# Two batches' loads cut into half-runs, and three loads issued later on GpSimd, in a cosine-weighted attention with adapter mixture

## The chip, the cores and the metric

The kernel runs on one core of one Trainium2 chip. The metric is the device time of one execution in microseconds (us); lower is better. Three runs of the kernel before gave 114.01, 114.30 and 114.53 us, so its median is 114.30 us.

## What is computed

Queries, keys and values have shape 8 x 8 x 576 x 64 (batch, heads, tokens, head size), in float32. Each batch goes through linear attention with cosine weights, and the 4608 tokens that come out, each of 512 numbers, go through a layer that picks the best two of eight small adapters:

```python
cos_w, sin_w = cos(pi/2 * pos / 576), sin(pi/2 * pos / 576)
phi(x) = concat([relu(x) * cos_w, relu(x) * sin_w])
kv  = einsum('bhsf,bhsd->bhfd', phi(k), v)      # 128 x 64 per head
z   = sum(phi(k), over s)
x   = (phi(q) @ kv) / (phi(q) @ z + 1e-6)       # tokens x 512
w   = softmax of the two largest of x @ w_gate  # 8 experts
out = x + sum over the two experts of w * (x @ A[e] @ B[e])
```

## The kernel before

**Batches and steps.** A batch's attention needs the whole of its keys and values first: `kv` sums over all its tokens. Only then can its queries be used. The kernel holds one batch as tiles of 128 partitions by 4 head pairs by 9 times 64 numbers: `rows` gives partition r of an even or odd head the nine tokens 9r to 9r+8, which lie next to each other in memory. So one load of k, q or v is 128 x 4 = 512 runs of 2304 bytes (576 float32 numbers), written as 1152 bytes of bfloat16. The nine tokens of a run are the "s values" 0 to 8 of the code.

The output is made in 36 tiles of 128 tokens. One loop, `for n in range(NT - 1)`, has a step for each tile; every engine runs its part of the step in the order in which the code writes it (the schedule is manual). Two batches share nine tiles. In step n VectorE (DVE) normalises tile n, TensorE (PE) transposes the queries of tile n+1, ScalarE (ACT) evacuates them, and the adapter stages of earlier tiles are mixed in.

**Keys.** Before PE can use the keys of a batch, each s value is turned into two scaled copies (`kp`, by cosine and sine). For batches 2 to 7 this is shared: DVE takes relu of the first part in place (`relu_k`, L165), GpSimd (POOL) then scales these s values two instructions each (L156, a "row" of GpSimd), DVE and ACT scale the rest from the raw keys (L153, L151). `pool_at`, `relu_at`, `dve_at` and `act_at` say in which step: batch 2 in step 5 with five s values on GpSimd, batch 3 in step 8 with seven, batch 4 in step 12 with eight, batch 5 in step 17 with eight, batches 6 and 7 in steps 20 and 23 with nine. In steps 5 and 8 DVE scales s value 7 first, by two L153 instructions, and then takes the two relus. PE uses the `kp` tiles in `kv` (L180), for batch 3 in the order 7, 0 | 1, 2, 3 | 4, 8, 6, 5 over steps 10, 11 and 12.

**Loads.** All loads but the first (batch 0's keys, on SyncE's queue) are issued by GpSimd, since they convert float32 to bfloat16. They use one DMA queue and land in the order of issue. In the built program the DMA starts of GpSimd take eight semaphores in turn, and each start waits until the eighth start before it has landed; GpSimd's later work stands behind such a wait. The order before is: v0, q0, k1, v1, q1, k2, three transfers of weights (A, w_gate and B, `load_weights`), v2, q2, k3, v3, k4, q3, v4, all written ahead of the loop; then behind each row of GpSimd the loads k(b+3), q(b+2), v(b+3). Here "k3" is batch 3's keys. The third and fourth batch of the change are batches 2 and 3 by this count.

**Stores.** SyncE waits for the last keys' load (`first_loads`, L570), stores the tiles held until then, and stores the others as they are made.

Of the kernel before, what the change touches and what calls it, by code (L numbers as in the profile page):

```python
# [19 lines left out]
def kernel(ctx, tc, q, k, v, w_gate, A, Bw, out):  # L20
# [27 lines left out]
    def rows(dram, b):  # L48
        return dram[b].rearrange("(g two) (r s) d -> (two r) g (s d)", two=2, s=NS)
# [9 lines left out]
    v_b += v_b[:3]  # L59

    def load(eng, t, dram, b):
        eng.dma_start(out=t, in_=rows(dram, b))  # L62

    def load_k(b, eng=None):
        load(eng or nc.gpsimd, k_b[b].rearrange("p g s d -> p g (s d)"), k, b)

    def load_q(b):
        load(nc.gpsimd, q_b[b].rearrange("p g s d -> p g (s d)"), q, b)

    def load_v(b):  # L70
        load(nc.gpsimd, v_b[b][:, 0:VN].rearrange("p (g x) -> p g x", g=G), v, b)
# [36 lines left out]
    def make_diag(s):  # L108
        for i, tab in enumerate((cos_tab, sin_tab)):
            nc.vector.tensor_scalar(out=diag[:, s, i], in0=ident, scalar1=tab[:, s:s + 1],  # L110
                                    scalar2=None, op0=ALU.mult)
# [6 lines left out]
    def load_weights():  # L118
        nc.gpsimd.dma_start(out=AW[:, 0:E].rearrange("p e c r -> p e (c r)"),
                            in_=A.rearrange("e (p c) r -> p e (c r)", c=DCH))  # L120
        nc.gpsimd.dma_start(out=AW[:, E, :, 0:E],
                            in_=w_gate.rearrange("(p c) e -> p c e", c=DCH))
        nc.gpsimd.dma_start(out=Ball, in_=Bw.rearrange("e r d -> (e r) d"))
# [35 lines left out]
    def scale_k(b, s, eng=("pool", "pool")):  # L159
        for i, e in enumerate(eng):  # L160
            scale_k1(b, s, i, e)
# [13 lines left out]
    def kv(b, s):  # L175
        first, last = kv_n[b] == 0, kv_n[b] == NS - 1
        kv_n[b] += 1
        for g in range(G):
            for par, pr in enumerate((lo, hi)):
                nc.tensor.matmul(out=kvz[par][:, g], lhsT=kp_t[b][pr, s, g],  # L180
                                 rhs=v_rhs(b, g, s, pr),
                                 start=(first and g == 0), stop=(last and g == G - 1))

    def kv_out(b):
        kv_t[b] = t = p_kv.tile([128, 2, G, W], BF16, name="kvsb")
        for par in range(2):
            src = kvz[par].rearrange("p g u d -> p g (u d)")[:, :, 0:W]
            nc.scalar.copy(t[:, par], src)
# [29 lines left out]
    def evac_q(n, gp, eng="act"):  # L218

        t = p_qpt.tile([128, 4, 128], BF16, name="qpT")  # L220
        src, qpT_t[n, gp] = qpT_t[n, gp], t
        if mixed(n):
            src = src.rearrange("p j h r -> p h j r")
            t = t.rearrange("p h (j r) -> p h j r", j=2)
        else:
            src = src.rearrange("p j h r -> p h r j")
            t = t.rearrange("p h (r j) -> p h r j", j=2)
        if eng == "act":
            nc.scalar.activation(t, src, AF.Relu)  # L229
        else:  # L230
            nc.vector.tensor_scalar(out=t, in0=src, scalar1=0.0, scalar2=None, op0=ALU.max)  # L231

    def move_q(n):
        transp_q(n)
        evac_q(n, 0)
        evac_q(n, 1)
# [148 lines left out]
    def delta(n, own=True):  # L385
        delta_x(n, own)
        delta_z(n)

    def delta_add(n, own=True):

        if own:
            dx = cd[dx_n[0] % 2]
            dx_n[0] += 1
        else:
            dx = qd.tile([128, DM], FP32, name="dx", tag="qd")
        g = group_of[n]
        nc.tensor.matmul(out=dx, lhsT=zgT_t[g][:, n - groups[g][0], :], rhs=Ball,
                         start=True, stop=True)
        osb_t[n] = dx
        evac_o(n)  # L400
        t = osb_t[n]
        nc.gpsimd.tensor_tensor(out=t, in0=t, in1=xt_t.pop(n), op=ALU.add)  # L402
# [77 lines left out]
    with tc.manual_schedule():  # L480
        for s in range(6):
            make_diag(s)
        wu = qd.tile([128, DM], FP32, name="wu", tag="qd")
        for i in range(24):
            nc.tensor.matmul(out=wu, lhsT=ones, rhs=wide, start=True, stop=True)  # L485
        for s in range(NS):
            scale_k(0, s, ("act" if s < 7 else "dve", "dve"))
            kv(0, s)
        nc.scalar.activation(warm, halfpi, AF.Sigmoid)
        for s in range(6, NS):  # L490
            make_diag(s)
        load_k(1)
        load_v(1)
        load_q(1)
        load_k(2)
        load_weights()
        load_v(2)
        load_q(2)
        load_k(3)
        load_v(3)  # L500
        load_k(4)
        load_q(3)
        load_v(4)
        kv_out(0)
        transp_q(0)
        evac_q(0, 0, "dve")
        evac_q(0, 1)
        numden(0)

        g10, g11, g12 = range(len(groups) - 3, len(groups))  # L510
        todo, held = [], []
        first_loads = persist.tile([1, 8], BF16, name="first_loads")

        def emit(d, own=True, eng="act", add=False):
            if add:
                delta_add(d, own)
            else:
                delta(d, own)
                evac_o(d, eng)
            if held is None:  # L520
                store(d)
            else:
                held.append(d)

        for n in range(NT - 1):
            if n > 0:
                g = move_at.get(n - 1, (None,))[0]
                evac_x(n - 1, g)
                if g is not None:
                    todo += groups[g]  # L530
            normalise(n)
            if n != 3:
                move_q(n + 1)
            for b, s in kv_at.get(n, ()):
                kv(b, s)
                if kv_n[b] == NS:
                    kv_out(b)
            for t in early_at.get(n, ()):
                logits(t)
            if n == 3:  # L540
                move_q(n + 1)
            for g in gate_a_at.get(n, ()):
                gate_a(g)
            for g in gate_b_at.get(n, ()):
                gate_b(g)
            now = todo[:2 if len(todo) > 3 and n not in kv_at else 1]
            del todo[:len(now)]
            for d in now:
                emit(d, n not in kv_at, add=n > 27)
            for g in gate_a_at.get(n, ()):  # L550
                gate_sig(g)
            transp_x(n)
            for g in move_at.get(n, ()):
                transp_z(g)
            for b, s, i in dve_at.get(n, ()):
                scale_k1(b, s, i, "dve")
            for b, s0, s1 in relu_at.get(n, ()):
                relu_k(b, s0, s1)
            for b, s in pool_at.get(n, ()):
                scale_k(b, s)  # L560
                if (b, s) == pool_at[n][-1]:
                    if b + 3 < B:
                        load_k(b + 3)
                    if b + 2 < B:
                        load_q(b + 2)
                    if b + 3 < B:
                        load_v(b + 3)
                    if b + 3 == B - 1:

                        nc.sync.dma_start(out=first_loads, in_=k_b[B - 1][0:1, 0, 0, 0:8])  # L570
                        for d in held:
                            store(d)
                        held = None
            for t in late_at.get(n, ()):
                logits(t)
            numden(n + 1)
            for b, s, i in act_at.get(n, ()):
                scale_k1(b, s, i, "act")


        evac_x(NT - 2)
        normalise(NT - 1)
        transp_z(g10)
        logits(NT - 2)
        evac_z(g10, [("act", 0, 3)])
        todo += groups[g10]
        for d in todo[:-3]:
            emit(d)
        transp_x(NT - 1)
        gate_a(g11)  # L590
        emit(todo[-3])
        gate_sig(g11)
        evac_x(NT - 1)
        logits(NT - 1)
        gate_b(g11)
        emit(todo[-2])
        gate_a(g12)
        transp_z(g11)
        evac_z(g11, [("act", 0, 2)])
        gate_sig(g12)  # L600
        emit(todo[-1])
        gate_b(g12)
        emit(NT - 3)
        transp_z(g12)
        evac_z(g12, [("dve", 0, 1)])
        emit(NT - 2)
        emit(NT - 1, eng="dve")
# [28 lines left out]
```

## Time and profile before

| | before |
|---|---|
| median of three runs | 114.30 us (114.01 to 114.53) |
| the profiled execution, its own time | 114.54 us |
| its span, first to last instruction | 112.8 us |
| granted TensorE clock | 0.996 |
| PE busy | 96.1 us (85%) |
| DVE busy | 83.7 us (74%) |
| ACT busy | 78.2 us (69%) |
| POOL busy | 72.3 us (64%) |
| GpSimd's DMA queue | 13856 packets, 13.84 MB |
| SyncE's DMA queue | 5792 packets, 10.62 MB |

Busy times leave out waiting and the issuing of DMAs where the profile gives that to a queue; GpSimd's own DMA starts (about 0.75 us each) are counted as busy. A busy PE is not PE at its peak. Times in the views count from the first instruction; 1.7 us of the execution lie outside the span.

### The profile page before, as it was taken

How to read it: one execution, taken by the hardware profiler on the slowest of the kernel's cores; microseconds unless marked ns; L12 is line 12 of the kernel's file. 1: busy time of each engine (PE TensorE's matmuls, PEld its weight loads, DVE VectorE, ACT ScalarE, POOL GpSimd, SP SyncE). 2: the span in 40 equal slices, each digit the busy share in tenths (PEclk: the TensorE clock that was granted, in tenths of full speed). 3: DMA queues.
4: the chain of work that ended last, by engine and by line, in shares of the span. 5: the costliest groups of instructions: out<-in, count | busy, mean ns of one | idle time of the engine just before them, and what ended most of it. 6: DMA issues, size and time to landing. Idle time of an engine off the chain costs nothing.

```text
span 112.8 us, 4956 instructions
## 1 busy us (share of the span) xinstructions
PE 96.1 (85%) x2050; PEld 74.1 (66%) x2068; DVE 83.7 (74%) x296; ACT 78.2 (69%) x169; POOL 72.3 (64%) x134
## 2 busy tenths in 40 slices
PE   2999676978899899999999999998998997978710
PEld 1347465867796788868788888785786886754200
DVE  5598489459969677695987998999949589786620
ACT  5087579755986595797876978856777777895720
POOL 5992223228995996299939999989980445774000
PEclk9999999999999999999999999999999999999998
DMA  2999999999999999999999999999999424526892
GB/s 41 385 206 208 213 202 210 210 180 208 208 208 209 207 209 209 209 206 213 204 207 208 208 209 208 242 348 383 381 324 366 142 100 97 185 101 226 285 340 82
DMA packets 19670, 24.77 MB, mean 220 GB/s; under 512 B 2624, under 2 KB 14528, under 8 KB 19648
## 3 DMA queue, kind: packets, MB, share of 16 engines
q0 software_dynamic: 13856, 13.84, 73.8%
q1 hardware_dynamic: 5792, 10.62, 26.9%
q8 instruction: 16, 0.26, 0.9%
q14 instruction: 6, 0.05, 0.1%
HBM read 28.85 MB, written 9.44 MB: 340 GB/s over the span
## 4 chain that ended last, share of the span: by engine, by line
PE 40%; DMA 28%; DVE 15%; issue 4%; POOL 4%; ACT 4%; POOLq 0%; DVEq 0%; ACTq 0%
DMA k<-in_k_dram 14%; DMA v<-in_v_dram 12%; PE cd L180 9%; PE za L311 7%; PE qd L213 6%; PE xz L285 5%; PE nd L257 4%; DVE xt L277 4%; PE dx L377 3%; DVE k L165 3%; DVE xT L291 2%; DVE zg L346 2%; ACT osb L408 2%; PE qd L201 2%; DMA out_dram<-osb 2%
## 5 line engine op out<-in xcount | busy, mean ns | idle before, releaser
L229 ACT ACTIVATE qpT<-qd 128x512 bf16<-128x512 f32 x71 | 38.6, 595 | 15.0 <-PE qd L213 10.9
L156 POOL TENSOR_SCALAR kp<-k,cos_tab 128x256 bf16<-128x256 bf16 x46 | 22.6, 490 | 7.1 <-DVE k L165 6.5
L277 DVE TENSOR_TENSOR xt<-nd,rden 128x512 bf16<-128x512 f32 x36 | 24.9, 691 | 1.3
L291 DVE COPY xT<-xz 128x512 bf16<-128x512 bf16 (+1 forms) x36 | 17.1, 476 | 9.9 <-PE xz L359 6.4
L156 POOL TENSOR_SCALAR kp<-k,sin_tab 128x256 bf16<-128x256 bf16 x46 | 21.9, 476 | 0.0
L180 PE MATMUL cd<-v,kp 64*128 64x128 bf16 x576 | 20.3, 217 | 0.9 <-DVE kp L153 0.9
L285 PEld LDWEIGHTS <-xt 128*128 128x128 bf16 x144 | 10.8, 115 | 12.1 <-DVE xt L277 7.9
L285 PE MATMUL xz<-ident,xt 128*128 128x128 bf16 x144 | 14.4, 222 | 5.0 <-DVE xt L277 4.3
L180 PEld LDWEIGHTS <-kp 64*128 64x128 bf16 x576 | 16.3, 94 | 3.1 <-issue 0.9
L257 PE MATMUL nd<-kvsb,qpT 128*128 128x65 bf16 (+1 forms) x320 | 16.7, 195 | 1.1 <-DVE qpT L231 0.5
L213 PE MATMUL qd<-diag,q 128*64 128x128 bf16 x432 | 17.3, 222 | 0.3 <-DMA q<-in_q_dram 0.3
L402 POOL TENSOR_TENSOR osb<-osb,xt 128x512 f32<-128x512 f32 x8 | 9.2, 1160 | 9.6 <-ACT osb L408 8.0
L408 ACT COPY osb<-dx 128x512 f32<-128x512 f32 x19 | 11.2, 588 | 5.9 <-remote 2.1
L213 PEld LDWEIGHTS <-q 128*64 128x64 bf16 x432 | 13.1, 109 | 1.8 <-DMA q<-in_q_dram 0.5
L257 PEld LDWEIGHTS <-qpT 128*128 128x128 bf16 (+1 forms) x320 | 12.7, 100 | 1.9 <-ACT qpT L229 0.7
L311 PE MATMUL za<-AW,xT 128*128 128x144 bf16 x140 | 12.4, 227 | 0.7 <-DVE zg L346 0.5
L311 PEld LDWEIGHTS <-xT 128*128 128x128 bf16 x144 | 9.0, 98 | 3.2 <-DVE xT L291 1.0
L408 ACT COPY osb<-cd 128x512 f32<-128x512 f32 x16 | 9.1, 597 | 1.3 <-PE cd L382 1.3
L62 POOL DMA_DIRECT2D v<-in_v_dram x8 | 6.2, 778 | 5.2 <-DMA q<-in_q_dram 4.4
L485 PE MATMUL wu<-wide,ones 128*128 128x512 bf16 x24 | 7.3, 477 | 2.0 <-DVE AW L115 2.0
L62 POOL DMA_DIRECT2D q<-in_q_dram x8 | 6.1, 763 | 3.6 <-DMA k<-in_k_dram 3.6
L62 POOL DMA_DIRECT2D k<-in_k_dram x7 | 5.4, 771 | 3.9 <-DMA k<-in_k_dram 2.2
(75 smaller groups left out, 133.8 us busy)
## 6 DMA issues: line engine op xcount, KB each, us to landing
out_dram<-osb SPq DMA_DIRECT2D x32, 256.0 KB, 3.9
v<-in_v_dram POOLq DMA_DIRECT2D x8, 576.0 KB, 16.5
q<-in_q_dram POOLq DMA_DIRECT2D x8, 576.0 KB, 15.6
k<-in_k_dram POOLq DMA_DIRECT2D x7, 576.0 KB, 15.5
k0f<-in_k_dram SPq DMA_DIRECT2D x1, 1152.0 KB, 5.4
out_dram<-osb SPq DMA_DIRECT2D x8, 128.0 KB, 2.4
AW<-in_moe_A_dram POOLq DMA_DIRECT2D x1, 128.0 KB, 18.2
Ball<-in_moe_B_dram POOLq DMA_DIRECT2D x1, 128.0 KB, 16.7
```

The source lines that it names most:

```text
L62: eng.dma_start(out=t, in_=rows(dram, b))
L156: nc.gpsimd.tensor_scalar(out=dst, in0=src, scalar1=tab, scalar2=1.0, op0=ALU.mult, op1=ALU.mult)
L180: nc.tensor.matmul(out=kvz[par][:, g], lhsT=kp_t[b][pr, s, g], rhs=v_rhs(b, g, s, pr), start=(first and g == 0), stop=(last and g == G - 1))
L213: nc.tensor.matmul(out=t[cols, j, 2 * gi:2 * gi + 2, :], lhsT=q_b[b][:, 2 * gp + gi, s, :], rhs=diag[:, s, i], start=(j == 0 and gi == 0), ...
L229: nc.scalar.activation(t, src, AF.Relu)
L257: nc.tensor.matmul(out=nd[pr, gg, j * W:(j + 1) * W], lhsT=qpT[:, j, pr], rhs=kv_t[b][:, h % 2, h // 2, :], start=(eps_dve(n) and j == 0), ...
L277: nc.vector.tensor_tensor(out=x, in0=nd[:, :, :, 0:D], in1=rden.rearrange("p (g j) -> p g j", g=2).to_broadcast([128, 2, 4, D]), op=ALU.mult)
L285: nc.tensor.transpose(out=xz[:, c * 128:(c + 1) * 128], in_=x[:, c], identity=ident)
L291: nc.vector.tensor_copy(t[:, 0:c], xz[:, 0:c * 128].rearrange("p (c s) -> p c s", c=c))
L311: nc.tensor.matmul(out=za_t[g][:, i, :], lhsT=xT[:, c, :], rhs=AW[:, :, c, :], start=(c == 0 and i == 0), stop=(c == DCH - 1), skip_group_ ...
L402: nc.gpsimd.tensor_tensor(out=t, in0=t, in1=xt_t.pop(n), op=ALU.add)
L408: nc.scalar.copy(t, src)
```

## The change

A load of batch 2 or 3 becomes two transfers. Each takes one half of every run: 512 pieces of 1152 bytes read and 576 written, first the numbers 0 to 287 of all runs (s values 0 to 3 and half of 4), then the others. This touches k2, v2, q2, k3, v3 and q3. The loads k4, q3 and v4 are taken from the list ahead of the loop and put behind GpSimd's row of batch 2, in step 5, ahead of the loads k5, q4 and v5 that stood there already.

GpSimd's order in the changed program: v0, q0, k1, v1, q1, k2 (two), A, w_gate, B, v2 (two), q2 (two), k3 (two), v3 (two); row of batch 2; k4, q3 (two), v4, k5, q4, v5; row of batch 3; the rest as before. The waits on the eighth start before stay and count the halves singly. DVE, ACT and PE keep their instructions and their order; what needs s values of one half only waits for that half.

```diff
     def load(eng, t, dram, b):
-        eng.dma_start(out=t, in_=rows(dram, b))
+        x = rows(dram, b)
+        if b in (2, 3):
+
+            t = t.rearrange("p g (h x) -> p h g x", h=2)
+            x = x.rearrange("p g (h x) -> p h g x", h=2)
+            for h in range(2):
+                eng.dma_start(out=t[:, h], in_=x[:, h])
+        else:
+            eng.dma_start(out=t, in_=x)
...
         load_q(2)
         load_k(3)
         load_v(3)
-        load_k(4)
-        load_q(3)
-        load_v(4)
         kv_out(0)
...
             for b, s in pool_at.get(n, ()):
                 scale_k(b, s)
                 if (b, s) == pool_at[n][-1]:
+                    if b == 2:
+                        load_k(4)
+                        load_q(3)
+                        load_v(4)
                     if b + 3 < B:
                         load_k(b + 3)
```

## The prediction

> **What bounds the kernel now.** I read the page first (engines, DMA, chain), then the chain of waits in order of time, then the stretches, then the timelines around the change. From the page:
>
> ```profile
> DMA  2999999999999999999999999999999424526892
> GB/s 41 385 206 208 213 202 210 210 180 208 208 208 209 207 209 209 209 206 213 204 207 208 208 209 208 242 348 383 381 324 366 142 100 97 185 101 226 285 340 82
> DMA packets 19670, 24.77 MB, mean 220 GB/s; under 512 B 2624, under 2 KB 14528, under 8 KB 19648
> ```
>
> Each figure stands for 2.82 us. From about 5.6 us to 70 us the DMA engines never pause, at a level 208 GB/s; one slice is at 180. A load of 576 KB (589,824 bytes) thus passes every 2.84 us, and each lands that much behind the one before it. The chain, in order of time, shows when this queue sets the pace:
>
> ```profile
> 4.62 13.85 DMA v<-in_v_dram
> 18.76 15.64 DMA k<-in_k_dram
> 34.42 0.48 DVE kp L153 x2
> 34.90 0.60 DVE k L165 x2
> 35.51 0.53 DVE xT L291
> ```
>
> The chain lies on loads until 34.40 us, when k3 lands and DVE, which scales k3's s value 7 first in step 8, can go on. What the wait itself is worth is in the waits of 26 to 36 us:
>
> ```profile
> DVE kp L153 <- DMA k<-in_k_dram: 0.2, 1, 0.2
> POOL kp L156 <- DVE k L165: 1.7, 2, 1.2
> ```
>
> DVE stood idle for only 0.2 us there. An earlier k3 brings 0.2 us at most, a later k3 costs all its delay. Behind that point the stretches say that nothing takes up such a delay:
>
> ```profile
> 20.00:22.50 2.50, 2.37 (x69) 1.99 (x65) 1.30 (x4) 1.84 (x6) 0.74 (x1) 1.00 1.22 213
> 22.50:25.40 2.90, 2.06 (x55) 1.73 (x57) 1.64 (x5) 1.71 (x4) 0.82 (x2) 1.00 1.78 180
> 25.40:30.00 4.60, 3.67 (x88) 3.15 (x82) 4.26 (x19) 3.17 (x8) 4.15 (x9) 1.00 1.21 207
> 40.00:50.00 10.00, 9.83 (x207) 7.78 (x209) 7.60 (x28) 7.61 (x18) 6.85 (x13) 1.00 1.21 208
> 60.00:70.00 10.00, 9.80 (x211) 8.10 (x212) 8.97 (x33) 7.68 (x18) 9.96 (x22) 1.00 1.21 207
> ```
>
> Columns: length; busy us of PE, weight loads, DVE, ACT, POOL; clock; DMA share; GB/s. From 40 us PE is busy 9.8 of every 10 us, in a fixed order, so what PE starts later ends later.
>
> **The half-runs on the DMA queue.** The bytes stay; k2, v2, q2, k3 ahead of k3's landing, and v3 and q3 behind it, take 512 more packets each, 32 on each of 16 engines. No packet of 576 bytes is in the trace. The nearest rows are the small ones of the weights:
>
> ```profile
> AW<-in_moe_A_dram POOLq DMA_DIRECT2D x1, 128.0 KB, 18.2
> AW<-in_moe_w_gate_dram POOLq DMA_DIRECT2D x1, 8.0 KB, 17.5
> ```
>
> A comes in runs of 64 numbers (128 bytes written), so 1024 packets; w_gate in runs of 8 (16 bytes), so 512. Both pass in the stretch 22.5 to 25.4, which moved 2.9 x 180 = 522 KB; at 208 GB/s that takes 2.51 us, so 0.39 us went to 1536 small packets, 96 on each engine: 4.1 ns for each. 32 of them make 0.13 us for a split load. Had the weights' 139 KB (0.67 us at 208 GB/s) cost nothing, it would be (0.39 + 0.67) / 96 = 11 ns, or 0.36 us. Zero is the other end: the same bytes at the same rate. I take 0.2 us, nearer to 0.13 since the small packets' bytes must have cost something. Four splits put k3's second half at 34.40 + 0.8 = 35.2 us; the ends are 34.4 and 35.8. s value 7 lies in the second half, so the early first half of k3 serves nobody: DVE waits in order for 7 before its relus. q2's and v2's first halves do land earlier, but the rows between 26 and 36 us hold no wait for q or v, so that gains nothing.
>
> The Trainium skill has a rule that speaks against the halves ("DMA: Bandwidth & Descriptors", How a descriptor splits into AXI transactions): a piece that does not begin on a 256-byte boundary pays for the bytes below its start. By that page's counting a run of 2304 bytes is 72 beats and its halves 36 and 40, an estimate of 4/72 of 2.84 us or 0.16 us more per split load, beside any cost per packet; four of them would put the sum 0.6 us higher. No run here shows it, since no row of this trace has such a start.
>
> **The three loads moved, and GpSimd's time.** GpSimd's timeline before:
>
> ```profile
> 24.53 0.74 POOL L62 DMA_DIRECT2D k<-in_k_dram  x1 [2.19 <-DMA k<-in_k_dram]
> 25.32 0.74 POOL L62 DMA_DIRECT2D q<-in_q_dram  x1
> 26.06 0.75 POOL L62 DMA_DIRECT2D v<-in_v_dram  x1
> 27.25 0.48 POOL L156 TENSOR_SCALAR kp<-k,cos_tab 128x256 bf16<-128x256 bf16 x1 [0.45 <-DVE k L165]
> 31.36 0.47 POOL L156 TENSOR_SCALAR kp<-k,sin_tab 128x256 bf16<-128x256 bf16 x1
> 33.30 0.76 POOL L62 DMA_DIRECT2D v<-in_v_dram  x1
> 35.28 0.58 POOL L156 TENSOR_SCALAR kp<-k,cos_tab 128x256 bf16<-128x256 bf16 x1 [1.21 <-DVE k L165]
> 41.30 0.48 POOL L156 TENSOR_SCALAR kp<-k,sin_tab 128x256 bf16<-128x256 bf16 x1
> 47.15 0.64 POOL L156 TENSOR_SCALAR kp<-k,cos_tab 128x256 bf16<-128x256 bf16 x1 [3.15 <-DVE k L165]
> ```
>
> Before, row 2 (from 27.25 us) stands behind 16 DMA starts; k4, the 14th, had to wait until the sixth, k2, landed. After, it stands behind 18: three go, five halves come. So the move does not free GpSimd. k3's first half is now the 15th start and waits for the seventh, k2's second half: 24.53 + 0.2 = 24.7 us; three more starts of 0.75 us (the last waits for B, which lands just before v2 begins, three loads ahead of k3: 34.40 - 3 x 2.84 = 25.9, plus 0.2 for k2, no hindrance) end at 27.7. Row 2 starts at 27.75 instead of 27.25 and ends at 32.3. Then come seven starts instead of three: k4 32.3, q3 33.05 and 33.8, v4 34.55, k5 35.3, q4 36.05, and v5, which waits for the eighth before it, v3's first half: 35.2 + 1.5 = 36.7, so it ends at 37.6. Row 3 starts at 37.7 instead of 35.28, 2.4 us late.
>
> Who waits for that? The DMA queue does not run dry: at 32.3 us, with k4's start, it still has k3 and v3 before it, to about 38. Row 4 waited 3.15 us for DVE before: row 3 now ends at 44.2, and its three loads at 46.5, still ahead of 47.15. PE is next, with batch 3's products:
>
> ```profile
> 33.10 1.29 PE L180 MATMUL cd<-v,kp 64*128 64x128 bf16 x40
> 39.32 0.62 PE L180 MATMUL cd<-v,kp 64*128 64x128 bf16 x16
> 41.69 0.84 PE L180 MATMUL cd<-v,kp 64*128 64x128 bf16 x24
> 44.59 1.07 PE L180 MATMUL cd<-v,kp 64*128 64x128 bf16 x32
> ```
>
> An s value is two instructions of 0.46 us on GpSimd and eight matmuls on PE. Batch 3: s value 0 is ready at 37.7 + 1.0 = 38.7, wanted behind 7 at 39.6; 3 at 41.4, wanted at 42.2; 6 at 44.2, wanted behind 4 and 8 at 45.1. Batch 2: 4 at 32.3, wanted behind 3 at 33.4. All hold by 0.8 us or more, and PE will itself be later. So the late rows cost nothing, while that cover of about 0.8 us lasts.
>
> **DVE beside GpSimd's DMA starts.** DVE's short instructions on bfloat16 in SBUF slow down while GpSimd works:
>
> ```profile
> 26.16 0.28 DVE L153 TENSOR_SCALAR kp<-k,cos_tab 128x256 bf16<-128x256 bf16 x1
> 26.35 0.51 DVE L153 TENSOR_SCALAR kp<-k,sin_tab 128x256 bf16<-128x256 bf16 x1
> 34.62 0.28 DVE L153 TENSOR_SCALAR kp<-k,sin_tab 128x256 bf16<-128x256 bf16 x1
> 34.82 0.69 DVE L165 TENSOR_SCALAR k<-k 128x768 bf16<-128x768 bf16 x2
> 65.87 1.30 DVE L165 TENSOR_SCALAR k<-k 128x768 bf16<-128x768 bf16 x2
> 73.57 2.36 DVE L165 TENSOR_SCALAR k<-k 128x768 bf16<-128x768 bf16 x2
> ```
>
> One instruction of two took 0.51 instead of 0.28 us beside v4's start at 26.06; in step 8 (34.42 on) GpSimd was idle, v5's start having ended at 34.06, and nothing was slowed. After, step 8's four instructions, from 35.2 on, run beside the starts of k5 and q4. Two starts at 0.23 us each are 0.46; none is the lower end; 1.30 against 0.69, the pair that met a start and a row, gives 0.6 as the upper. I take 0.3, on the path, right behind k3's wait. Step 5's four meet one start more than before (0.2), but that is ahead of k3's wait and hidden in it. The 2.36 us at 73.57 lie beside row 6 on GpSimd. That row follows row 5 without a gap (POOL busy 9.96 of 10 us from 60 on), and row 5 waits for DVE's own relu of step 17; both shift together, so I leave it.
>
> **The sum.** 0.8 (0 to 1.4) and 0.3 (0 to 0.6): +1.1 us, ends 0 and 2.0. On the profiled execution, 114.54 us (112.8 span and 1.7 around it), that is 115.6; on the median of the runs, 114.3, which lies 0.24 lower, it is 115.4. The queue ends 1.2 us later, six splits at 0.2, and the held stores with it; SyncE stored earlier tiles then, and PE's order does not wait for them.
>
> **Rivals.** *No change.* Half packets cost only their bytes, and DVE slips between the starts: 114.3 us. For it: the queue moves 213 and 207 GB/s around small packets. Against: the 180 slice. 114.1 to 114.8.
>
> *Faster.* k2's and k3's halves and a later k4 would have to free something on the path. The wait for k3 gives back 0.2 us and step 5's slowed instructions 0.2 more, if k3 came 0.4 us earlier: 113.9. It decides if half packets flow faster than whole ones; no row says so. A larger gain needs the 2.36 us at 73.57 to fall to about 1.0, if row 6 ended 1.4 us sooner against DVE: 113.0.
>
> *GpSimd's rows bind.* If GpSimd's starts take longer or its waits stack up, so that row 3 starts over 0.8 us behind my 37.7 with PE on its old times, PE waits for `kp` in steps 10 to 12. A row that starts two more us late gives about 1.2 us on top: 116.6. For it: the eight in flight are now halves. Against: every wait above ends before GpSimd gets there but v5's.
>
> *The change doesn't do what it says* holds in part within the forecast: GpSimd's row 2 starts later, not earlier.
>
> **How the numbers follow.** 0.5% (0.57 us) is about what a measurement of this kernel tells from no change. Forecast 0.65, of which 0.60 lies above 114.87 us and 0.05 below; no change 0.18; faster 0.11, of which 0.10 for the larger gain, since the small one of 0.4 us stays within 0.5%; rows bind 0.06. So faster 0.10, same 0.05 + 0.18 + 0.01 = 0.24, slower 0.60 + 0.06 = 0.66. The range goes from the no-change case, 114.2, to the sum's upper end, 114.3 + 2.0, with 0.1 on top for the ends' rounding: 116.4. It leaves out the larger gain, the worst of the rows, and little else.
>
> **What would show it.** Right: the slices from 16 to 34 us at 195 to 205 GB/s instead of 208; DVE's wait for k in step 8 at 0.8 to 1.2 us, the chain passing k3 at about 35.2; DVE's four instructions of step 8 at 1.5 us together; row 2 at 27.7 and row 3 at 37.7 on GpSimd; no wait of PE for GpSimd's `kp`. Wrong: k3 landing at 34.4 as before, a gap in the DMA row between 30 and 50 us, or PE waiting at L180 for POOL.

## The result, and the profile after

The changed kernel takes 115.29 us (five runs, 115.14 to 115.76) against 114.30 us before: a ratio of 1.0087, 95% interval 1.0067 to 1.0108, so 1.0 us slower. Run once more, it took 115.13 against 114.39: 1.0069 (1.0056 to 1.0082), 0.8 us. The profiled execution took 115.14 us, with a span of 113.4 us, against 114.54 and 112.8. The profile before had been one of the kernel's longer runs, which is why the two profiles differ by only 0.6.

The page after:

```profile
GB/s 38 387 208 208 207 208 207 201 177 203 194 200 199 206 204 205 213 204 208 208 207 207 207 209 207 272 294 371 389 354 356 172 98 93 184 106 223 284 335 87
DMA packets 22838, 24.77 MB, mean 218 GB/s; under 512 B 2720, under 2 KB 17696, under 8 KB 22816
```

The bytes are the same; 3168 more packets are the 6 x 512 of the half-runs and 96 of the six transfers' ends. The GB/s row reads 194 to 206 from the tenth slice to the sixteenth, while half-runs pass, where it read 207 to 209 before. One of the stretches shown before and the two behind it, up to step 8 (columns as there):

```profile
25.40:30.00 4.60, 3.66 (x86) 3.11 (x80) 4.36 (x18) 3.25 (x8) 4.59 (x10) 1.00 1.41 199
30.00:34.40 4.40, 4.40 (x123) 3.99 (x118) 3.10 (x12) 3.63 (x9) 4.40 (x8) 1.00 1.42 202
34.40:40.00 5.60, 4.04 (x78) 3.26 (x77) 4.16 (x12) 2.84 (x8) 5.08 (x10) 1.00 1.30 201
```

The last two in the profile before:

```profile
30.00:34.40 4.40, 4.40 (x123) 3.96 (x118) 3.19 (x12) 3.66 (x9) 4.07 (x8) 1.00 1.22 212
34.40:40.00 5.60, 4.78 (x93) 3.88 (x95) 4.51 (x15) 3.45 (x9) 4.72 (x11) 1.00 1.20 205
```

The queue runs at 199, 202 and 201 where it ran at 207, 212 and 205, 2 to 5% slower, and PE has 1.56 us of idle time in the third stretch instead of 0.82. The chain, in order of time:

```profile
6.84 17.55 DMA k<-in_k_dram
...
25.41 9.34 DMA k<-in_k_dram
34.78 0.54 DVE kp L161 x2
35.31 0.87 DVE k L173 x2
36.19 0.53 DVE xT L299
...
108.22 0.69 DVE osb L418
```

Its shape is the one from before: loads up to k3, then DVE's step 8, then PE. DVE goes on at 34.78 instead of 34.42 (0.36 later), is through with step 8's four instructions at 36.19 instead of 35.51 (0.68 later), and that difference stays almost to the last digit: tile 9 is normalised 0.67 us late, tile 22 0.66 and the last, at 102 us, 0.60. Behind step 8 no tile moves by more than 0.08 us against this. All of the change in these two profiles is made by the end of step 8. DVE there, and GpSimd around it:

```profile
34.78 0.47 DVE L161 TENSOR_SCALAR kp<-k,cos_tab 128x256 bf16<-128x256 bf16 x1 [0.65 <-DMA k<-in_k_dram]
34.98 0.33 DVE L161 TENSOR_SCALAR kp<-k,sin_tab 128x256 bf16<-128x256 bf16 x1
35.23 0.95 DVE L173 TENSOR_SCALAR k<-k 128x768 bf16<-128x768 bf16 x2
```

```profile
27.65 0.52 POOL L164 TENSOR_SCALAR kp<-k,cos_tab 128x256 bf16<-128x256 bf16 x1
...
34.41 0.78 POOL L70 DMA_DIRECT2D v<-in_v_dram  x1
35.14 0.79 POOL L70 DMA_DIRECT2D k<-in_k_dram  x1
35.88 0.80 POOL L70 DMA_DIRECT2D q<-in_q_dram  x1
...
37.94 0.49 POOL L164 TENSOR_SCALAR kp<-k,cos_tab 128x256 bf16<-128x256 bf16 x1
...
47.82 0.64 POOL L164 TENSOR_SCALAR kp<-k,cos_tab 128x256 bf16<-128x256 bf16 x1 [1.29 <-DVE k L173]
```

DVE's wait for k3 grew from 0.21 to 0.65 us. Its four instructions span 1.41 us instead of 1.09, beside the starts of v4, k5 and q4. GpSimd's row 3 starts 2.7 us late, but ahead of row 4 GpSimd still waits 1.29 us for DVE's relu, so its own delay is gone by then.

### The profile page after: what moved, and what is told of

Same layout as the page of the kernel before. It is cut to its first block, busy times and chain, and to the rows that moved or that the text cites. A ratio compares the mean times of both kernels' runs of the same rounds, so it can differ in the third digit from the quotient of the medians.

```text
span 113.4 us, 4962 instructions
## 1 busy us (share of the span) xinstructions
PE 96.7 (85%) x2050; PEld 74.2 (65%) x2068; DVE 83.9 (74%) x296; ACT 78.2 (69%) x169; POOL 76.5 (67%) x140
## 4 chain that ended last, share of the span: by engine, by line
PE 42%; DMA 26%; DVE 14%; POOL 6%; issue 4%; ACT 4%; POOLq 0%; DVEq 0%; ACTq 0%
DMA k<-in_k_dram 24%; PE cd L188 9%; PE za L319 7%; PE qd L221 6%; PE xz L293 5%; PE nd L265 4%; DVE xt L285 4%; DVE k L173 3%; PE dx L385 3%; DVE xT L299 2%; ACT osb L416 2%; PE qd L209 2%; DMA out_dram<-osb 2%; DVE zg L354 2%; PE cd L385 2%
## 5 line engine op out<-in xcount | busy, mean ns | idle before, releaser
L493 PE MATMUL wu<-wide,ones 128*128 128x512 bf16 x24 | 7.8, 500 | 2.0 <-DVE AW L123 2.0
L278 DVE RECIPROCAL rden<-nd 128x8 f32<-128x8 f32 x20 | 4.1, 204 | 4.1 <-PE nd L265 3.9
L493 PEld LDWEIGHTS <-ones 128*128 128x128 bf16 x24 | 2.9, 121 | 6.4 <-issue 3.7
L354 DVE TENSOR_TENSOR zg<-za,em 128x384 bf16<-128x384 f32 (+1 forms) x12 | 6.6, 546 | 0.4
```

## The experiments

Two costs are in question, the half packets on the queue and GpSimd's starts beside DVE's step 8, against a third, GpSimd's late rows. Each kernel below takes out one or more. "Go" is the time at which DVE starts step 8's first instruction; "four" the time from there to the end of the second relu (1.09 us before).

**The halves alone, without the move** (edit against the changed kernel).

```diff
         load_k(3)
         load_v(3)
+        load_k(4)
+        load_q(3)
+        load_v(4)
...
-                    if b == 2:
-                        load_k(4)
-                        load_q(3)
-                        load_v(4)
```

> The halves alone: six loads cut in two, k4, q3 and v4 stay ahead of GpSimd's row of batch 2. Two-cost theory (half packets cost 0.5 us on the queue ahead of k3, GpSimd's starts beside DVE's step 8 cost 0.3): these stay, but now row 2 stands behind 22 starts, and v4's start waits for q2's second half (about 32 us), so the row starts at about 32.8 instead of 27.65. Its s value 0 is then ready at 33.8 where PE wants it at 30.4, and s value 4 at 37.4 where PE wants it at 33.4: 3.4 to 4 us later, 118 us (117.3 to 119). Rival, the place of the three loads doesn't matter since GpSimd's rows have room: as the changed kernel, 115.3.

121.34 us, ratio 1.0579 (1.054 to 1.0618): 6.9 us slower, nearly twice what was expected. PE's products of batch 2 in step 7:

```profile
30.18 0.40 PE L188 MATMUL cd<-v,kp 64*128 64x128 bf16 x8
...
33.97 0.61 PE L188 MATMUL cd<-v,kp 64*128 64x128 bf16 x8 [3.38 <-POOL kp L164]
...
34.87 0.61 PE L188 MATMUL cd<-v,kp 64*128 64x128 bf16 x8 [0.30 <-POOL kp L164]
...
35.78 0.61 PE L188 MATMUL cd<-v,kp 64*128 64x128 bf16 x8 [0.29 <-POOL kp L164]
```

and the stretches (the value before DMA's share is PE's clock):

```profile
26.00:30.00 4.00, 3.20 (x70) 2.85 (x72) 3.73 (x17) 2.87 (x8) 3.19 (x5) 1.00 1.41 199
30.00:34.00 4.00, 0.62 (x20) 0.35 (x16) 1.30 (x3) 2.62 (x7) 2.50 (x5) 0.78 1.41 198
34.00:36.50 2.50, 1.91 (x26) 1.18 (x27) 0.00 (x0) 0.00 (x0) 2.50 (x6) 0.50 1.41 201
36.50:40.00 3.50, 3.50 (x62) 3.32 (x62) 1.49 (x6) 0.57 (x2) 3.26 (x6) 0.63 1.26 208
```

The expected wait is there: row 2 starts at 32.98 behind 22 starts, and PE waits 3.38 + 0.30 + 0.29 = 4.0 us for `kp`. What was not expected is the clock: while PE was idle for 3.4 us it fell to 0.50, and PE did its next steps slowly (eight products in 0.61 instead of 0.40 us). A mean of 0.78 over the 4 us from 30 to 34 is 1.8 us at 0.50, so the clock fell at about 32.2 us, 1.7 us behind the end of PE's last product (30.58); by the last stretch's 0.63 it was back at about 39.1. The Trainium skill ("TensorE: Matmul & The Clock Gate", Part 1: The HAM clock gate) tells of half the clock after an idle window of about 3.4 us. Here it came after 1.7 us of idle time, so this trace does not bear that figure out. The move of the three loads is therefore no decoration of the change: with the halves, it is what keeps row 2 in time.

**The move alone, without the halves.**

```diff
     def load(eng, t, dram, b):
-        x = rows(dram, b)
...
+        eng.dma_start(out=t, in_=rows(dram, b))
```

> The move alone: no load is cut. Two-cost theory: k3 lands as before; row 2 starts at about 26.9 (before 27.25); the starts of k4, q3, v4, k5, q4, v5 run from 31.4 to 36, so the last two stand beside DVE's step 8 as in the changed kernel: 0.3 us more, less 0.1 for a quieter step 5: 114.5 (114.3 to 114.7). Queue theory (all of the 1.0 us is half packets): 114.2. Starts theory (all is GpSimd's starts beside DVE): 115.0 to 115.3. Late-row theory (row 3 behind more starts costs): row 3 starts at 36 instead of 35.3, about 0.2: 114.5.

114.90 us against 114.42, ratio 1.0043 (1.0027 to 1.0059): 0.5 us slower: above the 114.3 to 114.7 expected from two costs, and below the 115.0 expected if all of it were GpSimd's starts. DVE in step 8:

```profile
34.31 0.29 DVE L153 TENSOR_SCALAR kp<-k,cos_tab 128x256 bf16<-128x256 bf16 x1 [0.19 <-DMA k<-in_k_dram]
34.52 0.28 DVE L153 TENSOR_SCALAR kp<-k,sin_tab 128x256 bf16<-128x256 bf16 x1
34.71 0.88 DVE L165 TENSOR_SCALAR k<-k 128x768 bf16<-128x768 bf16 x2
```

k3's landing is as before, the wait 0.19 us; the four span 1.28 us, beside the starts of q4 and v5 (34.48 to 36.1). So starts beside step 8 cost time with whole loads too. This profile is the shortest of the kernel's twelve runs (114.58 to 115.46), so the 0.2 us that it shows is less than the typical cost; what the longer runs met is in no profile.

**Halves by head pairs.** As many starts in the same places as in the changed kernel, but whole runs:

```diff
         if b in (2, 3):
-
-            t = t.rearrange("p g (h x) -> p h g x", h=2)
-            x = x.rearrange("p g (h x) -> p h g x", h=2)
             for h in range(2):
-                eng.dma_start(out=t[:, h], in_=x[:, h])
+                gp = slice(2 * h, 2 * h + 2)
+                eng.dma_start(out=t[:, gp], in_=x[:, gp])
```

> The changed kernel with its loads cut in two by head pairs and not within the runs: the same number of starts in the same places, but 512 packets of 1152 bytes for a load as before. Two-cost theory: k3 lands 0.4 to 0.5 us earlier than in the changed kernel, the 0.3 beside DVE's step 8 stays: 114.8 (114.6 to 115.0). Queue theory: 114.3. Starts theory and late-row theory: 115.3, as changed.

115.12 us against 114.42, 1.0073 (1.005 to 1.0095), not apart from the changed kernel by its interval: inconclusive by time. The four span 1.28 us, with one instruction at 0.56 beside a start, and k3 was waited for no more: in this profile DVE's own chain was late (go at 34.47, right behind its work of step 7). Part of the time is none of either theory's: this kernel has 2.0 us outside its span, 114.96 against 112.9, where the others have about 1.8, and the other kernel cut by heads, below, has it again.

**Quiet step 8, with the halves.** The changed kernel, with v4, k5, q4 and v5 started behind row 3:

```diff
                     if b == 2:
                         load_k(4)
                         load_q(3)
+                    if b == 3:
                         load_v(4)
+                        load_k(5)
+                        load_q(4)
+                        load_v(5)
-                    if b + 3 < B:
+                    if b != 2 and b + 3 < B:
...
```

> The changed kernel with the starts of v4, k5, q4 and v5 moved behind GpSimd's row of batch 3, so that no start stands beside DVE's four instructions of step 8, and row 3 starts at about 36 instead of 37.9. The halves stay. Two-cost theory: 0.3 us less than the changed kernel: 115.0 (114.8 to 115.1). Queue theory: 115.3. Starts theory: 114.4. Late-row theory: 114.5 to 114.8.

115.38 us, 1.0086 (1.0064 to 1.0107): no gain. Its profile showed k3 landing later than in any other profile (go at 35.46), so it was run again beside others:

> The kernel with quiet step 8 and halves a second time, since its first run gave 115.4 where the two-cost theory had 115.0. Its first profile shows DVE's four instructions of step 8 at 1.09 us as before, a later step 12 (+0.13, its relus now meet GpSimd's starts), and k3's landing 13.96 us behind q1's, against 13.39 in the changed kernel and 12.82 before. If that landing was one draw's scatter: 13.4 again, and 115.0 to 115.2 us. If it belongs to the kernel: 13.9 again, and 115.4.

115.10 us against 114.44, 1.0062 (1.0048 to 1.0075). The late landing did not come back; the second profile:

```profile
34.76 0.28 DVE L161 TENSOR_SCALAR kp<-k,cos_tab 128x256 bf16<-128x256 bf16 x1 [0.69 <-DMA k<-in_k_dram]
34.96 0.28 DVE L161 TENSOR_SCALAR kp<-k,sin_tab 128x256 bf16<-128x256 bf16 x1
35.16 0.69 DVE L173 TENSOR_SCALAR k<-k 128x768 bf16<-128x768 bf16 x2
...
47.03 0.88 DVE L173 TENSOR_SCALAR k<-k 128x768 bf16<-128x768 bf16 x2
...
50.50 0.93 PE L188 MATMUL cd<-v,kp 64*128 64x128 bf16 x16
```

Go at 34.76, as in the changed kernel, and the four back at 1.08: with no start beside them they run as before. Tile 9 comes 0.33 us late instead of 0.67, so the starts' share in step 8 is 0.3 us, and the rest is the queue's. By time, though, no gain can be told from the changed kernel's second run (1.0069, 1.0056 to 1.0082). Part of it is given back: the starts now meet DVE's relus of step 12 (0.88 us instead of 0.75, 0.13 on the path). Another 0.31 us is lost ahead of tile 15 in this profile, where PE's first products of batch 4 take 0.93 us, with no wait on record. In the first profile of the same kernel they take 0.62:

```profile
51.21 0.62 PE L188 MATMUL cd<-v,kp 64*128 64x128 bf16 x16
```

So this stall belongs to the one execution and not to the kernel; its cause is open.

**The changed kernel again.** No edit:

> The changed kernel once more, beside the others on one chip: 115.3 (115.1 to 115.5) by every theory. Its profile is a second draw of the delay at k3's landing (0.36 us later than before in the first profile, 0.5 expected) and of DVE's step 8 (1.33 us against 1.09 before in the first profile, 1.2 to 1.6 expected).

115.13 us against 114.39, as above. The second profile agrees with the first in the sum and not in its parts: tile 9 is 0.65 us late, of which go (34.89) has 0.47 and the four (1.28 us) 0.19. DVE's wait for k3 is only 0.37 us in it, because DVE's own chain was late as well.

**Both costs out.** By heads and quiet (the two edits above together), and whole loads and quiet:

> Both suspected costs taken out at once: loads cut by head pairs (whole runs, so no more packets) and the starts of v4, k5, q4 and v5 behind GpSimd's row of batch 3 (no start beside DVE's step 8). The number of starts ahead of the row of batch 2 stays at 18. Two-cost theory: as before, 114.4 (114.2 to 114.6). Third-cost theory (the starts ahead of step 8 slow the chain itself, or the late rows or later loads cost): 0.4 to 0.8 stay, 114.8 to 115.2.

> No load cut; k4 and q3 behind GpSimd's row of batch 2, and v4, k5, q4, v5 behind its row of batch 3. The kernel before with its GpSimd free of starts in steps 5 and 8. Two-cost theory: 114.3 (114.0 to 114.5), k3's wait of 0.2 us stays. Third-cost theory, if the cost lies in the later starts of v4 to v5: 114.8 or more; if it lies in the number of starts ahead of row 2, 114.3.

By heads: 114.87 against 114.39, 1.0045 (1.0033 to 1.0057), of which about 0.2 us is again the time outside the span (114.97 less 113.0). Whole: 114.65, 1.0023 (1.0014 to 1.0032). Both lie above what two costs alone would leave (114.4 and 114.3), and share a third cost, that of the later starts: the four are at 1.09 us in both, but the relus of step 12 meet starts, as in the quiet kernel with halves. With whole loads:

```profile
46.52 0.88 DVE L165 TENSOR_SCALAR k<-k 128x768 bf16<-128x768 bf16 x2
```

against `46.70 0.75` before. Against the quiet kernel with halves (1.0062), the whole loads differ in the cut alone: 0.0039 of 114.4, or 0.45 us, to within about 0.2. Against the one cut by heads they differ by 0.0022, or 0.25 us, most of which is the 0.2 outside the span; by time, then, the half packets cost more than the cut as such.

**Past k3.** Two attempts to beat both kernels, from the kernel just shown (whole loads, quiet step 8). `load_weights` is given a part, 0 for A and w_gate and 1 for B; B, needed at 36 us first, is loaded behind k3:

```diff
         load_k(2)
-        load_weights()
+        load_weights(0)
...
         load_k(3)
+        load_weights(1)
         load_v(3)
```

> The kernel c1 with the weights B loaded behind k3 instead of ahead of v2: k3 lands 0.6 us earlier, B still lands at about 34.8, ahead of its first use at 36.3. If k3's landing paces steps 1 to 8 and nothing stands right behind it, 0.2 to 0.6 us less than c1; if DVE's own chain is as late as k3 (its wait was only 0.2 us), 0.2 less: 114.1 (113.8 to 114.3).

114.45 against 114.39, 1.0007 (0.999 to 1.0025), where 114.1 was expected. k3 came 0.6 us sooner than in that kernel and nobody waited for it any more: go at 33.92. In the profile tile 9 is 0.51 us early and the run is 0.45 us shorter than before (114.09). But the twelve runs spread from 114.09 to 115.41, where those of before lie within 0.3 us. In the last kernel, v4's start stands behind row 2 again:

> The kernel c2 (no load cut, B behind k3, GpSimd free in step 8) with v4's start put back behind the row of batch 2, so that six starts instead of seven stand behind the row of batch 3 and none meets DVE's relus of step 12. If those starts are what cost 0.13 us in step 12, c2 less 0.13: 114.2 to 114.3 us, and 0.1 to 0.2 less than the kernel before. Rival, the start of v4 meets step 8: as c2 or 0.2 more, 114.5.

114.43 against 114.44, 1.0001 (0.998 to 1.0021), above the 114.2 to 114.3 expected. Step 12's relus are at 0.75 again, as expected. Five of its twelve runs are at 114.06 to 114.11, three above 114.8. In the profiled run (114.49) tile 0 is normalised 0.46 us late and tile 8 still 0.29, so go is at 34.41. A like lateness at tile 0, 0.5 to 0.6 us, is in three other profiles (the changed kernel's second, the halves by heads, the first of the quiet one with halves); in the first and third DVE still had to wait for k3, which hid it. With k3 out of the way, batch 0's stage sets the pace in this profile; what the longest runs met is in none. So neither is faster than the kernel before.

## Why the prediction was right

**The place.** Forecast was a delay made at k3's landing and in DVE's step 8 that nothing takes up behind. That is what the tiles show, 0.67 us at tile 9 and 0.60 at tile 35. 115.4 was forecast, 115.29 measured. That they lie within 0.1 us is in part luck: the queue term was too large by about as much as the terms, as measured, fall short of the time.

**The queue term was too large.** It was put at 0.2 us for a split load, 0.8 for four. GpSimd's start that waits for q1, the last load ahead of all splits, gives a mark common to the kernels (before, then changed):

```profile
21.60 0.74 POOL L62 DMA_DIRECT2D v<-in_v_dram  x1 [2.10 <-DMA q<-in_q_dram]
```

```profile
21.39 0.74 POOL L68 DMA_DIRECT2D q<-in_q_dram  x1 [2.08 <-DMA q<-in_q_dram]
```

From there to go it is 34.42 - 21.60 = 12.82 us before and 34.78 - 21.39 = 13.39 after: 0.57 us, 0.14 for a split load. The second profile of the changed kernel gives 34.89 - 21.54 = 13.35, and the second quiet one with halves 34.76 - 21.45 = 13.31; the first quiet one, with its late k3, gives 13.96. Whole loads stay at 12.81 and 12.82 (the move alone, and whole loads with a quiet step 8). So 0.12 to 0.14 for a split load is the lower reading of the small packets, 0.13 us, and the step from there to 0.2 was the mistake. Since q1 also landed 0.2 us sooner in the changed kernel's profile than in the one before, go moved by only 0.36: k3 let DVE go at 34.78, not 35.2, and DVE's wait was 0.65, below the 0.8 to 1.2 given.

Not all of the 0.57 need be the smaller packets: the prediction gave the second transfer of a load no price of its own. Cut by heads and quiet, with no packet smaller:

```profile
21.42 0.70 POOL L66 DMA_DIRECT2D q<-in_q_dram  x1 [2.14 <-DMA q<-in_q_dram]
34.53 0.29 DVE L159 TENSOR_SCALAR kp<-k,cos_tab 128x256 bf16<-128x256 bf16 x1 [0.46 <-DMA k<-in_k_dram]
```

That is 13.11 us, 0.29 more than before; in the other kernel cut by heads it is at most 34.47 - 21.48 = 12.99, where DVE did not wait. So by these profiles up to half of the 0.57 can lie in the cut as such; the rest is the half packets'. The Trainium skill's rule on pieces that begin off a 256-byte boundary ("DMA: Bandwidth & Descriptors", How a descriptor splits into AXI transactions) would have added an estimated 0.16 for each split to any cost per packet; the measured 0.14 holds both and is less than the 0.16 alone, so this case does not show it.

**The starts beside step 8 were sized right.** 0.3 forecast; the four grew by 0.32 in the first profile and by 0.19 in the second, and fell back to 1.08 and 1.09 us in each of the quiet kernels. Together they took 1.41 and 1.28 us, a little under the 1.5 given as a sign.

**GpSimd's rows.** Row 2 at 27.65 (27.7 forecast), row 3 at 37.94 (37.7), and PE's list of waits from 26 to 50 us has none for GpSimd's `kp`: the late rows cost nothing, and the rival "rows bind" fell here. (The list puts 0.8 us at 36.77 down to v3's landing, but the product that waits, L390, reads no v; in the profile before, the same product waited for DVE's reciprocal, which is later here with step 8.) The halves without the move show its price, and it was not remote: four starts more ahead of row 2, and it is 5.3 us late.

**The sum.** 0.57 and 0.19 to 0.32 make 0.8 to 0.9, against 1.0 and 0.8 in the two comparisons. The move alone costs 0.5 by time and only 0.2 by its one profile, so how the typical step 8 looks in that kernel, and what makes up the 0.2 us or so that the first comparison shows beyond the two terms, stay open.

## What to carry to other kernels

Before a load is cut in two, look which of its parts the first waiting instruction needs: DVE asked for s value 7 of k3 first, which lies in the second half, so the halves could only delay it. Count starts against the number that may be in flight, since each extra one pushes back the work queued behind it on its engine. And when starts are moved, look at what the other engine does at the new place: here they slowed DVE in step 8 or, moved on, in step 12; only in the last kernel, where they stood beside neither, did both run as before.

## What the runs showed of the hardware

- In a gap of 3.4 us PE's clock fell to 0.50, 1.7 us after PE's last product, and it stayed there for 6.9 us (32.2 to 39.1). PE waited 4.0 us in all, and 6.9 were lost.
- A load cut into half-runs, 512 packets more for the same bytes, cost 0.12 to 0.14 us on 16 engines in three profiles of four, at most 4.4 ns for each added packet of an engine. Cut by head pairs, with no smaller packets, a load cost up to 0.07 us.
- Four short DVE instructions on bfloat16 took 1.28 to 1.41 us beside GpSimd's DMA starts in four profiles of three kernels, and 1.08 to 1.09 without them in the eight other profiles: never a value between.
- Loads cut by head pairs left 2.0 us instead of 1.8 outside the span, in both kernels that did so; nothing here says why.
